# One statistics chain for the first tiles, upper parts written from x by VectorE, second halves normalised by ScalarE

## The chip, the core and the metric

The kernel runs on one core of one Trainium2 chip. The metric is the time of one execution on the device in microseconds (us). The engines of the core work side by side, each through its own instructions in order: TensorE (PE; its weight loads are shown apart as PEld), VectorE (DVE), ScalarE (ACT), GpSimd (POOL) and SyncE (SP), whose queue issues most of the DMAs.

## The reference

`x` has 2048 rows of 512. Its normalised rows go through two branches, and the product of these is added to `x`:

```
def reference(x, seq_re, seq_im, hid_re, hid_im, w1, b1, w2, b2):
    xn = (x - mean(x)) / sqrt(var(x) + 1e-5)          # over the 512 columns
    a, b = xn @ hid_re.T, xn @ hid_im.T
    s = seq_re @ a - seq_im @ b                       # seq: 2048 x 2048, hid: 512 x 512
    h = relu(xn @ w1 + b1) ** 2                       # 512 -> 1792
    g = silu(h @ w2 + b2)                             # 1792 -> 512
    return x + s * g
```

All of it is in float32.

## The kernel before

**Products of split numbers.** A float32 product is made of three products of float32r operands: each operand is split into an upper part (`HI`, the value written to a float32r tile, which rounds it) and a lower part (`LO`, the value minus its upper part), and upper x upper, upper x lower and lower x upper are summed in PSUM (`PASSES`, L98). `split_hi` (L133) is an ACT copy, `split_lo` (L136) a DVE subtraction.

**Chunks and steps.** The kernel first multiplies the sequence matrices with `xn`, in eight chunks of 256 output rows. A chunk has eight steps `j`; step `j` uses the tile pair `xr[j]`, rows 128 j and 1024 + 128 j onwards (the two halves `h` = 0 and 1), and a piece of the sequence matrices, loaded into `raw[c, j]` (tag `u`, three buffers) and split into `part[c, j]` (tags `ga`, `gb`). The first two chunks (`PLAIN`) are plain products: `products(c, j, h)` issues 12 matmuls of 128 x 512 for each half, four accumulators for each of the three passes, so 24 a step. In the first chunk the passes go one after the other over the four accumulators, so the lower parts are needed later than the upper. The later chunks use seven products of sums in place of eight (`PRODUCTS`); for these, `XC[j]` holds besides the four plain blocks also three blocks of sums of the blocks of `xn` (S2 to S4), and S1 in the place of a plain block.

**The first chunk also normalises.** While PE multiplies step `j`, the other engines prepare step `j + 1`. On DVE's and ACT's queues, step by step (L515 to L536):

- `ln_rstd(j)` (L223): from the root that ACT left, a RECIPROCAL and three small DVE operations make 1 / sqrt(var + eps) with one Newton step.
- `ln_xn(j, h)` (L232): DVE normalises each half into `xn32[j]` (tiles `wd0` for j = 0 to 3, `wd1` for 4 to 7); ACT writes the upper part of each into `XC[j]`.
- `split_lo(*g)`: DVE's lower part of this step's `g`; then `load_c` and some `load_x` on SP's queue, which wait until buffers are free.
- `split_lo` of `XC[j]`, half 0; then the statistics of tile `j + 1`: half 0 on DVE (`ln_stats`), half 1 on ACT (`ln_mean`, `ln_var`: a pass for the mean, one for the squares), and both roots by one ACT operation (`ln_root`); then `split_lo` of half 1.
- From `j = 5` on (`NJ - 3`), one item of `aside`; then the products; then ACT's upper part of the next `g`.

**The list `aside`** (L511) is work for later chunks, taken item by item: four sums over `xn32[0..3]` (`sums(0)`, DVE, 1024 columns), a split of the sums of each of these four tiles (`split_sums`: an ACT write of 768 columns, then a DVE subtraction), the same for tiles 4 to 7, and weights. What the first chunk doesn't take is taken beside the second chunk (`beside`, a budget of `ASIDE` for each step). `sums` writes in place over `xn32`, so it needs all four tiles of its group done and split.

**The start** (L475 to L506). PE is kept busy by 8 narrow-type and 6 float32r matmuls on zeros (`WARM`). For tile 0, each half has its own statistics and root; ACT splits the first half of `g`, DVE normalises, ACT writes the upper part from `xn32`, and the rest follows in an order written out by hand. All order here is the program's order: each engine runs its instructions as they are written.

Of the kernel before, what the change touches and what calls it, by code (L numbers as in the profile page):

```python
# [10 lines left out]
AF = mybir.ActivationFunctionType  # L11
ALU = mybir.AluOpType

P = 128
S, D, F = 2048, 512, 1792
NS, ND, NF = S // P, D // P, F // P
NJ, NP = NS // 2, NF // 2
# [1 line left out]
NC = S // CW  # L19
TC = 512  # L20
NTC = S // TC
WARM = 8, 6
PLAIN = 2

ASIDE = 3.6

REST = NP - 4

# [68 lines left out]
HI, LO = 0, 1  # L97
# [31 lines left out]
def fnet_gated_kernel(ctx, tc, x, xt, ct, wd, w1, w2, b1, b2, out):  # L129
    nc = tc.nc  # L130
    ctx.enter_context(tc.manual_schedule(engines=None))

    def split_hi(hi, lo, src):  # L133
        nc.scalar.activation(hi, src, AF.Copy)  # L134

    def split_lo(hi, lo, src):  # L136
        nc.vector.tensor_tensor(lo, src, hi.bitcast(F32), op=ALU.subtract)  # L137
# [5 lines left out]
    def copy(to, src, scale=1.0):  # L143
        nc.scalar.activation(to, src, AF.Copy, scale=scale)
# [8 lines left out]
    stats = pool.tile([P, 2, 2, NJ], F32, name="stats")  # L153
# [14 lines left out]
    def buf(tag, shape, name, dtype=F32):  # L168
        return pool.tile(shape, dtype, tag=tag, bufs=3 if tag == "u" else 1, name=name)

    def operand_buf(tag, name, step, shape=(2, 7, 256)):

        first = START.get(tag, 0)
        skip = (step - first) % 4 * LANE
        size = shape[0] * shape[1] * shape[2]
        room = ROOM.get(tag, 0)
        flat = buf(tag, [P, size + (room or skip)], name, F32R)
        a, b, c = shape
        return flat[:, skip:skip + size].rearrange("p (a b c) -> p a b c", a=a, b=b, c=c)

    def bcast(src, n):
        return bass.AP(tensor=src.tensor, offset=src.offset, ap=[[0, P], [1, n]])

    def halves(ap):
        return ap.rearrange("p (a b) -> p a b", a=2)


    XC = [None] * NJ
    for j in (0, 4, 5, 6, 7, 1, 2, 3):
        XC[j] = operand_buf(f"xc{j}", f"xc{j}", 3 if j in TURNED else 1, (7, 2, 256))  # L190
    small = buf("e", [P, 3, 16], "small")

    X_ROOM = "pq00", "pq01", "pq10", "pq11", "pq00", "pq01", "pq11", "pq00"
    xr, xn32 = {}, {}

    def load_x(j, hs=slice(0, 2)):

        if j not in xr:
            xr[j] = buf(X_ROOM[j], [P, 2, D], f"x{j}")
        nc.sync.dma_start(xr[j][:, hs], x.rearrange("(h j p) d -> j p h d", h=2, p=P)[j][:, hs])  # L200

    def ln_stats(j, h=0):
        bn = small[:, j % 3, 6 * h:6 * h + 6]
        nc.vector.bn_stats(bn, xr[j][:, h])
        nc.vector.bn_aggr(stats[:, :, h, j], bn)

    def ln_mean(j, h):

        nc.scalar.activation(junk, xr[j][:, h], AF.Copy, scale=1.0 / D, accum_out=stats[:, 0, h, j:j + 1])

    def ln_var(j, h):

        total = small[:, j % 3, 6 * h:6 * h + 1]
        nc.scalar.activation(junk, xr[j][:, h], AF.Square, bias=stats[:, 0, h, j:j + 1], scale=-1.0, accum_out=total)
        copy(stats[:, 1, h, j:j + 1], total, 1.0 / D)
# [3 lines left out]
    def ln_root(j, hs=slice(0, 2)):  # L219
        root[j] = small[:, j % 3, 12:16].rearrange("p (a h) -> p a h", a=2)  # L220
        nc.scalar.activation(root[j][:, 0, hs], stats[:, 1, hs, j], AF.Sqrt, bias=eps)

    def ln_rstd(j, hs=slice(0, 2)):  # L223
        y, q = root[j][:, 0, hs], root[j][:, 1, hs]
        var = rstd = stats[:, 1, hs, j]
        nc.vector.reciprocal(y, y)

        nc.vector.scalar_tensor_tensor(q, var, EPS, y, op0=ALU.add, op1=ALU.mult)
        nc.vector.scalar_tensor_tensor(q, q, -0.5, y, op0=ALU.mult, op1=ALU.mult)
        nc.vector.scalar_tensor_tensor(rstd, q, 1.5, y, op0=ALU.add, op1=ALU.mult)  # L230

    def ln_xn(j, h):  # L232
        if j % ND == 0 and h == 0:
            xn32[j, "tile"] = buf(f"wd{j // ND}", [P, ND, 2, D], f"xn32_{j}")
        if h == 0:
            xn32[j] = xn32[j // ND * ND, "tile"][:, j % ND]
        nc.vector.tensor_scalar(xn32[j][:, h], xr[j][:, h], stats[:, 0, h, j:j + 1], stats[:, 1, h, j:j + 1],
                                op0=ALU.subtract, op1=ALU.mult)

    def xc_parts(j, h):  # L240
        s = slice(2 * h, 2 * h + 2)
        return XC[j][:, s, HI, :], XC[j][:, s, LO, :], halves(xn32[j][:, h])
# [26 lines left out]
    def load_c(c, j, hs=slice(0, 2)):  # L269
        if (c, j) not in raw:  # L270
            raw[c, j] = buf("u", [P, 8, CW], f"u{c}_{j}")
        q = slice(2 * hs.start, 2 * hs.stop)
        nc.sync.dma_start(raw[c, j][:, q], ct[c, j, :, q])

    def plain_parts(c, j, hs=slice(0, 2)):
        if (c, j) not in part:
            part[c, j] = operand_buf("g" + "ab"[j % 2], f"g{c}_{j}", 0 if (c, j) == (PLAIN - 1, NJ - 1) else 3 if j in TURNED else 1, (2, 4, CW))
        g, r = part[c, j], raw[c, j]
        s = slice(2 * hs.start, 2 * hs.stop)
        return g[:, HI, s], g[:, LO, s], r[:, s]  # L280
# [87 lines left out]
    def products(c, j, h):  # L368

        for passes in [PASSES] if c else [[q] for q in PASSES]:  # L370
            for k in range(ND):
                one_product(c, j, h, k, passes)
# [8 lines left out]
    one, two = slice(0, 1), slice(1, 2)  # L381
# [95 lines left out]
    idle = buf("wd1", [P, 768], "idle")  # L477
    for count, zeros in zip(WARM, (idle[:, 0:256].bitcast(mybir.dt.bfloat16), idle[:, 256:768])):
        nc.vector.memset(zeros, 0.0)
        if zeros.dtype == F32:  # L480
            zeros = zeros.bitcast(F32R)
        for _ in range(count):
            nc.tensor.matmul(warm, zeros[:, 0:P], zeros, start=True, stop=True)
    for h, hs in enumerate((one, two)):
        ln_stats(0, h)
        ln_root(0, hs)
    split_hi(*plain_parts(0, 0, one))
    ln_rstd(0, one)
    ln_xn(0, 0)
    split_hi(*xc_parts(0, 0))  # L490
    split_lo(*plain_parts(0, 0, one))
    split_hi(*plain_parts(0, 0, two))
    ln_rstd(0, two)
    ln_mean(1, 1)
    ln_xn(0, 1)
    split_hi(*xc_parts(0, 1))
    split_lo(*xc_parts(0, 0))
    ln_stats(1)
    ln_var(1, 1)
    ln_root(1)  # L500
    split_lo(*plain_parts(0, 0, two))
    split_lo(*xc_parts(0, 1))
    g = plain_parts(0, 1)
    split_hi(*g)
# [9 lines left out]
    load_x(4)  # L514
    for j in range(1, NJ):  # L515
        ln_rstd(j)
        for h in range(2):
            ln_xn(j, h)
            split_hi(*xc_parts(j, h))
        split_lo(*g)  # L520
        load_c(*order[j + 3])
        if j in (1, 3, 4):
            load_x({1: 5, 3: 6, 4: 7}[j])
        split_lo(*xc_parts(j, 0))
        if j + 1 < NJ:
            ln_stats(j + 1)
            ln_mean(j + 1, 1)
            ln_var(j + 1, 1)
            ln_root(j + 1)
        split_lo(*xc_parts(j, 1))  # L530
        if j >= NJ - 3:
            next(aside)
        for h in range(2):
            products(0, j, h)
        g = plain_parts(*order[j + 1])
        split_hi(*g)  # L536
        if j == 2:
            nc.sync.dma_start(b1s, b1)
            nc.sync.dma_start(b2s, bcast(b2, D))
# [5 lines left out]
    def beside(spent):  # L545
        while spent < ASIDE:
            spent += next(aside, ASIDE)

# [47 lines left out]
    for n, s in enumerate(steps):  # L596
        c, j = s
# [3 lines left out]
        g = part.pop(s)  # L601
# [553 lines left out]
def _launch(arrays, out_shape):  # L1155
    import numpy as np
    import concourse.bacc as bacc
    from concourse.bass_utils import run_bass_kernel_spmd

    nc = bacc.Bacc("TRN2", target_bir_lowering=False, num_devices=1, dynamic_dma_scratch_size=1024)  # L1160
    feed, args = {}, []
    for name, v in arrays.items():
        v = np.ascontiguousarray(v)
        feed[f"in_{name}"] = v
        args.append(nc.dram_tensor(f"in_{name}", v.shape, mybir.dt.from_np(v.dtype), kind="ExternalInput").ap())
    args.append(nc.dram_tensor("out_0", out_shape, F32, kind="ExternalOutput").ap())
    with tile.TileContext(nc, schedule_with_timeline_sim=True) as tc:
        fnet_gated_kernel(tc, *args)
    r = run_bass_kernel_spmd(nc, [feed], core_ids=[0])
    return r.results[0]["out_0"]  # L1170
# [25 lines left out]
```

## Time and profile before

| | us |
|---|---|
| median of 3 runs | 673.32 |
| lowest and highest run | 673.16, 674.82 |
| span of the profiled execution | 671.8 |

The page gives the span of the profiled execution, and no time of its own for what lies around it; the median of the runs is 1.5 us longer than the span. The page has the busy time of each engine, then tenths of busy time in 40 slices, the DMA queues, the chain of work that ended last, and the costliest groups of instructions. A row of the timeline has start, duration, engine, line, operation, what it writes and reads, and in brackets the idle time of the engine before it with what ended that. A row with "x2" holds two instructions, and its duration reaches from the start of the first to the end of the last. On DVE and ACT an instruction can start shortly before the one ahead has ended, so the distance of two starts is what an instruction costs its queue. The granted clock of PE was full in all slices:

```profile
PEclk9999999999999999999999999999999999999999
```

### The profile page before, as it was taken

Reading aid. Unit: us, or ns where it says so; the run is one execution under the profiler, and the core shown is the slowest. Engines: PE = TensorE matmul, PEld = TensorE weight load, DVE = VectorE, ACT = ScalarE, POOL = GpSimd, SP = SyncE. Lnnn points to the kernel's source line nnn. Section 1 sums busy time; section 2 is a strip of 40 time slices with the busy share of each in tenths; the row PEclk is TensorE's granted clock in tenths of the full one; section 3 lists DMA queues with packets and bytes.
Section 4 is the critical chain, followed back from the end, with each engine's and each line's share of the span. In section 5 each row is a group of like instructions: output and inputs, shape, how many; then the busy total and the mean of one; then the engine's idle time right before and its main releaser. Section 6 shows DMA issues by size and latency. Waiting matters only on the chain.

```text
span 671.8 us, 13185 instructions
## 1 busy us (share of the span) xinstructions
PE 666.4 (99%) x5438; PEld 647.1 (96%) x5438; DVE 597.3 (89%) x833; ACT 379.0 (56%) x524; POOL 8.8 (1%) x11
## 2 busy tenths in 40 slices
PE   9999999999999999999999999999999999999997
PEld 6888889999999999999999999999999999999997
DVE  7997878999999999799899988977887889999997
ACT  6856554534445354444365557788778765454451
POOL 0000000000000000000000000000000000101010
PEclk9999999999999999999999999999999999999999
DMA  8625767646556774759588658676755866766776
GB/s 304 213 98 216 252 237 279 214 148 213 209 166 228 252 282 158 265 174 350 184 299 269 199 188 300 196 267 210 267 185 196 324 240 214 184 227 181 228 205 156
DMA packets 51739, 150.82 MB, mean 224 GB/s; under 512 B 4960, under 2 KB 19552, under 8 KB 50272
## 3 DMA queue, kind: packets, MB, share of 16 engines
q1 hardware_dynamic: 43568, 129.28, 56.5%
q10 hardware_dynamic: 6208, 18.88, 7.1%
q0 software_dynamic: 1904, 1.84, 1.9%
q8 instruction: 42, 0.69, 0.4%
q14 instruction: 17, 0.14, 0.1%
HBM read 101.98 MB, written 47.99 MB: 223 GB/s over the span
## 4 chain that ended last, share of the span: by engine, by line
PE 97%; DVE 1%; DMA 1%; ACT 0%; issue 0%; SPq 0%; DVEq 0%
PE m L362 34%; PE m_o L861 15%; PE r_B L755 13%; PE r_A L755 9%; PE pq_b L377 8%; PE r_C L755 4%; PE r_D L755 4%; PE m_last L861 4%; PE pq_ba L377 2%; PE pq_bc L377 2%; PE pq_bb L377 2%; DMA u<-in_ct 1%; DVE z L1111 0%; DVE z L911 0%; DVE z L916 0%
## 5 line engine op out<-in xcount | busy, mean ns | idle before, releaser
L362 PEld LDWEIGHTS m<-g,xc 128*128 128x128 f32 x2016 | 229.1, 188 | 0.1
L362 PE MATMUL m<-g,xc 128*128 128x256 f32 x2016 | 229.1, 276 | 0.0
L134 ACT ACTIVATE g<-u 128x1792 fp32r<-128x1792 f32 (+2 forms) x65 | 99.0, 1523 | 132.5 <-PE m L362 92.6
L137 DVE TENSOR_TENSOR g<-u,g 128x1792 fp32r<-128x1792 f32 (+2 forms) x65 | 116.9, 1798 | 19.8 <-ACT g L134 19.2
L861 PE MATMUL m_o<-w,g 128*128 128x256 f32 x882 | 100.5, 276 | 0.0
L861 PEld LDWEIGHTS m_o<-w,g 128*128 128x128 f32 x882 | 100.3, 188 | 0.0
L134 ACT ACTIVATE g<-hr 128x1792 fp32r<-128x1792 f32 (+2 forms) x31 | 48.2, 1566 | 40.0 <-DVE hr L296 15.3
L755 PE MATMUL r_B<-xT,w 128*128 128x256 f32 x504 | 66.5, 276 | 0.0
L377 PE MATMUL pq_b<-g,xc 128*128 128x512 f32 x240 | 65.3, 391 | 0.2 <-ACT xc L134 0.2
L755 PEld LDWEIGHTS r_B<-xT,w 128*128 128x128 f32 x504 | 61.4, 188 | 0.0
L137 DVE TENSOR_TENSOR g<-hr,g 128x1792 fp32r<-128x1792 f32 (+2 forms) x31 | 56.7, 1838 | 3.0 <-ACT g L134 2.8
L377 PEld LDWEIGHTS pq_b<-g,xc 128*128 128x128 f32 x240 | 44.8, 188 | 10.9 <-ACT xc L134 1.1
L755 PE MATMUL r_A<-xT,w 128*128 128x256 f32 x336 | 43.1, 276 | 0.0
L755 PEld LDWEIGHTS r_A<-xT,w 128*128 128x128 f32 x336 | 40.3, 188 | 0.2 <-DVE xT L137 0.2
L755 PE MATMUL r_B<-wdp,yg 128*128 128x256 f32 x288 | 35.8, 276 | 0.0
L284 DVE TENSOR_TENSOR u<-u 128x512 f32<-128x512 f32 x48 | 32.9, 685 | 2.4 <-DMA u<-in_ct 2.4
L755 PEld LDWEIGHTS r_B<-wdp,yg 128*128 128x128 f32 x288 | 34.1, 188 | 0.0
L861 PE MATMUL m_last<-w,g 128*128 128x256 f32 x294 | 33.5, 276 | 0.0
L861 PEld LDWEIGHTS m_last<-w,g 128*128 128x128 f32 x294 | 33.4, 188 | 0.0
L137 DVE TENSOR_TENSOR yg<-yraw,yg 128x1792 fp32r<-128x1792 f32 x13 | 26.2, 2018 | 0.6 <-ACT yg L134 0.6
L134 ACT ACTIVATE yg<-yraw 128x1792 fp32r<-128x1792 f32 x13 | 22.2, 1711 | 6.9 <-DVE yraw L293 6.4
L755 PE MATMUL r_D<-xT,w 128*128 128x256 f32 x168 | 23.6, 276 | 0.0
(187 smaller groups left out, 878.1 us busy)
## 6 DMA issues: line engine op xcount, KB each, us to landing
u<-in_ct SPq DMA_DIRECT2D x63, 512.0 KB, 3.8
hd<-h ACTq DMA_DIRECT2D x28, 512.0 KB, 4.2
hr<-hd SPq DMA_DIRECT2D x28, 512.0 KB, 3.7
wdp<-wdd SPq DMA_DIRECT2D x8, 896.0 KB, 6.2
yraw<-pqd SPq DMA_DIRECT2D x13, 512.0 KB, 6.3
pqd<-c SPq DMA_DIRECT2D x6, 1024.0 KB, 6.5
w<-w1d SPq DMA_DIRECT2D x6, 896.0 KB, 9.0
y<-y ACTq DMA_DIRECT2D x8, 512.0 KB, 6.1
```

Source lines behind the costliest of these rows:

```text
L134: nc.scalar.activation(hi, src, AF.Copy)
L137: nc.vector.tensor_tensor(lo, src, hi.bitcast(F32), op=ALU.subtract)
L284: nc.vector.tensor_tensor(t[:, 0:2], r[:, 0:1].to_broadcast([P, 2, 256]), r[:, 1:3], op=ALU.add)
L362: nc.tensor.matmul(ps[:, d], w[:, a_, d * P:(d + 1) * P], halves(mv(b_)), start=first and d == 0 and (a_, b_) == (HI, HI), stop=last and ( ...
L377: nc.tensor.matmul(accs[c][k], w, part[c, j][:, b_, 2 * h:2 * h + 2], start=j == 0 and h == 0 and (a_, b_) == (HI, HI), stop=j == NJ - 1 a ...
L755: nc.tensor.matmul(self.region(REGION[k]), w, mv, start=i == 0 and k in (1, 7), stop=i == len(ops) - 1, skip_group_check=True)
L861: nc.tensor.matmul(m[:, i * 256:(i + 1) * 256], ready[n][:, a_, H_SLOT[a], i * P:(i + 1) * P], W2[p][:, b_, b], start=p == 0 and i == 0 an ...
```

## The change

At the start, both halves of tile 0 have their statistics first, and then one root and one chain of small operations for both. A new function `ln_hi` lets DVE write an upper part straight from `x` (subtract the mean, multiply, write to `XC`), without going through `xn32`. A new function `ln_xn_act` lets ACT normalise a half into `xn32` as scale * x + bias, for which `ln_shift` makes the bias, minus mean times scale, on DVE. In step 0, both upper parts come from `ln_hi`, both halves of `xn32` from ACT. In step 1, the upper part of half 0 comes from `ln_hi`, both halves of `xn32` from ACT, and the lower part of `g` is made in two pieces. In steps 2 to 7, DVE normalises half 0 and ACT half 1, and ACT writes both upper parts from `xn32` as before. `SIDE` takes items of `aside` in step 4 (one) and in steps 5, 6 and 7 (two each) instead of one in each of 5, 6 and 7. One warm-up matmul goes.

```diff
-WARM = 8, 6
+WARM = 8, 5
...
+SIDE = {4: 1, 5: 2, 6: 2, 7: 2}
...
+    def ln_shift(j):
+
+        t = small[:, j % 3, 8:10]
+        nc.vector.scalar_tensor_tensor(t, stats[:, 0, :, j], -1.0, stats[:, 1, :, j], op0=ALU.mult, op1=ALU.mult)
+
+    def ln_xn_act(j, h):
+
+        xn32_tile(j, h)
+        nc.scalar.activation(xn32[j][:, h], xr[j][:, h], AF.Identity, scale=stats[:, 1, h, j:j + 1],
+                             bias=small[:, j % 3, 8 + h:9 + h])
+
+    def ln_hi(j, h):
+
+        nc.vector.tensor_scalar(XC[j][:, 2 * h:2 * h + 2, HI, :], halves(xr[j][:, h]), stats[:, 0, h, j:j + 1],
+                                stats[:, 1, h, j:j + 1], op0=ALU.subtract, op1=ALU.mult)
...
-    for h, hs in enumerate((one, two)):
-        ln_stats(0, h)
-        ln_root(0, hs)
+    for h in range(2):
+        nc.vector.bn_stats(small[:, 0, 6 * h:6 * h + 6], xr[0][:, h])
+    for h in range(2):
+        nc.vector.bn_aggr(stats[:, :, h, 0], small[:, 0, 6 * h:6 * h + 6])
+    ln_root(0)
+    ln_rstd(0)
+    ln_hi(0, 0)
+    ln_shift(0)
     split_hi(*plain_parts(0, 0, one))
-    ln_rstd(0, one)
-    ln_xn(0, 0)
-    split_hi(*xc_parts(0, 0))
+    split_hi(*plain_parts(0, 0, two))
     split_lo(*plain_parts(0, 0, one))
-    split_hi(*plain_parts(0, 0, two))
-    ln_rstd(0, two)
+    ln_xn_act(0, 0)
+    split_lo(*xc_parts(0, 0))
+    ln_hi(0, 1)
     ln_mean(1, 1)
-    ln_xn(0, 1)
-    split_hi(*xc_parts(0, 1))
-    split_lo(*xc_parts(0, 0))
+    ln_xn_act(0, 1)
     ln_stats(1)
     ln_var(1, 1)
+    split_lo(*plain_parts(0, 0, two))
     ln_root(1)
-    split_lo(*plain_parts(0, 0, two))
     split_lo(*xc_parts(0, 1))
...
     for j in range(1, NJ):
         ln_rstd(j)
-        for h in range(2):
-            ln_xn(j, h)
-            split_hi(*xc_parts(j, h))
-        split_lo(*g)
+        if j == 1:
+            ln_hi(j, 0)
+            ln_shift(j)
+            for h in range(2):
+                ln_xn_act(j, h)
+            split_lo(*plain_parts(0, j, one))
+            split_hi(*xc_parts(j, 1))
+            split_lo(*xc_parts(j, 0))
+            split_lo(*plain_parts(0, j, two))
+        else:
+            ln_shift(j)
+            ln_xn(j, 0)
+            ln_xn_act(j, 1)
+            for h in range(2):
+                split_hi(*xc_parts(j, h))
+            split_lo(*g)
+            split_lo(*xc_parts(j, 0))
         load_c(*order[j + 3])
...
-        split_lo(*xc_parts(j, 0))
...
         split_lo(*xc_parts(j, 1))
-        if j >= NJ - 3:
+        for _ in range(SIDE.get(j, 0)):
             next(aside)
```

More of the change, by code (lines that the diff above doesn't have):

```diff
@@ L230, in ln_rstd, with xn32_tile @@
         nc.vector.scalar_tensor_tensor(rstd, q, 1.5, y, op0=ALU.add, op1=ALU.mult)
+    def xn32_tile(j, h):
+        if j % ND == 0 and (j, "tile") not in xn32:
+            xn32[j, "tile"] = buf(f"wd{j // ND}", [P, ND, 2, D], f"xn32_{j}")
+        xn32[j] = xn32[j // ND * ND, "tile"][:, j % ND]
     def ln_xn(j, h):
[L233 to L236, printed above, removed]
+        xn32_tile(j, h)
         nc.vector.tensor_scalar(xn32[j][:, h], xr[j][:, h], stats[:, 0, h, j:j + 1], stats[:, 1, h, j:j + 1],
                                 op0=ALU.subtract, op1=ALU.mult)
+    def ln_shift(j):
+        t = small[:, j % 3, 8:10]
+        nc.vector.scalar_tensor_tensor(t, stats[:, 0, :, j], -1.0, stats[:, 1, :, j], op0=ALU.mult, op1=ALU.mult)
+    def ln_xn_act(j, h):
+        xn32_tile(j, h)
+        nc.scalar.activation(xn32[j][:, h], xr[j][:, h], AF.Identity, scale=stats[:, 1, h, j:j + 1],
[3 more added lines that the diff above has]
+                                stats[:, 1, h, j:j + 1], op0=ALU.subtract, op1=ALU.mult)
     def xc_parts(j, h):
```

## The prediction

> **What bounds the kernel now.** I read the page first, then the chain of work in order of time, then the waits of TensorE (PE), then VectorE (DVE) and ScalarE (ACT) row by row through the first 60 us, where the change lies.
>
> ```profile
> PE 666.4 (99%) x5438; PEld 647.1 (96%) x5438; DVE 597.3 (89%) x833; ACT 379.0 (56%) x524; POOL 8.8 (1%) x11
> ...
> PE warm L483 <- DVE idle L479: 1.2, 1, 1.2
> PE pq_b L377 <- ACT xc L134: 0.2, 1, 0.2
> ...
> 1.66 4.49 DMA u<-in_ct
> ...
> 6.17 0.63 ACT g L134
> 6.79 0.53 ACT xc L134
> ...
> 7.37 0.73 PE pq_b L377 x2
> ...
> 13.34 0.72 PE pq_b L377 x2
> ...
> 19.09 0.46 PE pq_b L377 x2
> ...
> 46.31 0.45 PE pq_b L377 x2
> ```
>
> The first row is busy time by engine; the next two are all the waits that PE has in the whole run, 1.2 us in front of the warm-up and 0.2 us at the first product; the rest are pieces of the chain (start, duration, what). The chain leaves the DMA of `u`, crosses two ACT splits, and is on PE from 7.37 us on. **So the time is the moment of PE's first product, plus what PE stands still, plus its work.** The most that a better start can give is small: the first product needs ACT's split of `u`, which starts at 6.17 us, so the gain there is under 1.2 us. What the change can lose has no such limit: each us that PE waits in the first chunk goes to the end, as nothing behind it waits today and so nothing gives way.
>
> Steps 2 to 7 of the first chunk take PE (46.31 - 19.09) / 5 = 5.44 us each. The question is whether the eight steps' operands still come in time. How far DVE and ACT are ahead today (start, duration, line, out<-in):
>
> ```profile
> 11.29 0.16 DVE L226 RECIPROCAL small<-small 128x2 f32<-128x2 f32 x1
> ...
> 16.12 0.16 DVE L226 RECIPROCAL small<-small 128x2 f32<-128x2 f32 x1
> ...
> 36.61 0.16 DVE L226 RECIPROCAL small<-small 128x2 f32<-128x2 f32 x1
> ...
> 37.39 1.00 DVE L237 TENSOR_SCALAR xn<-x,stats 128x512 f32<-128x512 f32 x2
> 38.31 1.22 DVE L137 TENSOR_TENSOR g<-u,g 128x1024 fp32r<-128x1024 f32 x1
> 39.44 0.69 DVE L137 TENSOR_TENSOR xc<-xn,xc 128x512 fp32r<-128x512 f32 x1
> 40.04 0.69 DVE L204 BATCH_NORM_STATS2 small<-x 128x6 f32<-128x512 f32 x1
> ...
> 40.87 0.66 DVE L137 TENSOR_TENSOR xc<-xn,xc 128x512 fp32r<-128x512 f32 x1
> 41.44 1.22 DVE L255 TENSOR_TENSOR xn<-xn 128x1024 f32<-128x1024 f32 x1
> 42.58 0.16 DVE L226 RECIPROCAL small<-small 128x2 f32<-128x2 f32 x1
> 43.36 1.00 DVE L237 TENSOR_SCALAR xn<-x,stats 128x512 f32<-128x512 f32 x2
> ...
> 43.94 1.16 ACT L134 ACTIVATE xc<-xn 128x512 fp32r<-128x512 f32 x2 [1.65 <-DVE xn L237]
> ```
>
> A step begins on DVE with its RECIPROCAL: step 1 at 11.29, 2 at 16.12, 6 at 36.61, 7 at 42.58 us. DVE has no gap between these rows. Step 7's first upper part is written by ACT at 43.94 + 0.61 = 44.55 us, and PE wants it at 46.31: **cover of 1.76 us at step 7**, with one sum (1.14 us from 41.44 to 42.58) in each of steps 5, 6 and 7.
>
> **The change part by part.**
>
> *The start.* Before, ACT wrote the first upper part behind the split of `u`; now DVE writes it from `x`.
>
> ```profile
> 3.52 0.69 DVE L204 BATCH_NORM_STATS2 small<-x 128x6 f32<-128x512 f32 x1 [1.82 <-DMA x<-in_x]
> ...
> 5.22 0.13 DVE L226 RECIPROCAL small<-small 128x1 f32<-128x1 f32 x1
> ...
> 5.97 0.55 DVE L237 TENSOR_SCALAR xn<-x,stats 128x512 f32<-128x512 f32 x1
> 6.17 0.63 ACT L134 ACTIVATE g<-u 128x512 fp32r<-128x512 f32 x1 [0.53 <-DMA u<-in_ct]
> ...
> 7.22 0.61 ACT L134 ACTIVATE g<-u 128x512 fp32r<-128x512 f32 x1
> ```
>
> One chain for both tiles: two statistics from 3.52, aggregates, one root, RECIPROCAL near 5.4, four small operations (5.22 to 5.97, 0.75) to 6.2, upper part by 6.75. The split of `u` ends at 6.80 and is last: first product near 6.85, 0.5 us sooner. The sixth wide warm-up matmul had to go for that. Dropping it costs nothing, since PE then has only a gap below 0.1 us.
>
> Behind it DVE forms the shift and one lower part, then waits for ACT's normalised half, which stands behind the second split of `u` (between 6.70, ACT free, and 7.22; I take 6.9) and ends near 8.25. Then lower part, upper part, statistics and two lower parts (0.60 + 0.46 + 0.82 + 1.20) bring step 1's RECIPROCAL to 11.4, against 11.29. **PE is 0.5 us earlier, DVE 0.1 us later.**
>
> *The normalisation on ACT.* No row has an ACTIVATE with two operands per partition (scale and bias). Nearest rows:
>
> ```profile
> 22.32 1.16 ACT L134 ACTIVATE xc<-xn 128x512 fp32r<-128x512 f32 x2 [0.51 <-DVE xn L237]
> 23.38 0.58 ACT L209 ACTIVATE junk<-x 128x512 f32<-128x512 f32 x1
> ...
> 24.97 0.20 ACT L144 ACTIVATE stats<-small 128x1 f32<-128x1 f32 x1
> 25.40 0.30 ACT L221 ACTIVATE small<-stats,eps 128x2 f32<-128x2 f32 x1 [0.23 <-DVE stats L205]
> ...
> L214 ACT ACTIVATE junk<-x,stats 128x512 f32<-128x512 f32 x7 | 4.8, 689 | 0.2
> L813 ACT ACTIVATE h<-h,b1s 128x512 f32<-128x512 f32 x10 | 7.1, 715 | 0.0
> ```
>
> A plain one takes 0.61 us, and the next starts 0.53 us after it; with one such operand it takes 0.69 to 0.715. If a second adds as much again, it is 0.77 to 0.82; I take 0.80, the next 0.71 later. The ends are 0.61 (free) and 0.82.
>
> In steps 2 to 7 ACT now runs: second half normalised (behind DVE's shift), both upper parts, mean, variance, root. From RECIPROCAL: 0.78 to the shift, 0.16 and a handover to 0.99, then 0.71 + 1.06 (two upper parts, 22.32 to 23.38) + 1.82 (23.38 to 25.17, and a handover) + 0.30 + 0.08 = **4.95 us to the next RECIPROCAL by ACT**. DVE's own: step 6 took 5.97, less a sum of 1.14, less one normalisation of 0.46, plus 0.08 for the shift = **4.45 us by DVE**. Without a sum the step is therefore 4.95, no shorter than the 4.83 it was: ACT's root is what is late next.
>
> Step 1 is longer, as both halves are on ACT and the shift stands behind DVE's upper part: 1.45 to ACT's start, 1.54 for two, 0.53, 1.82, 0.38 = 5.72. So step 2 starts at 11.4 + 5.72 = 17.1 instead of 16.12.
>
> Here a rule speaks against the change. The Trainium skill, "ScalarE: Activation LUTs", section "Rules for kernel authors", says that multiplying and adding belong on VectorE, not on ScalarE. The rows agree only where ACT sets the step: 0.46 us (37.39 to 38.31, two) leave DVE and some 0.71 come to ACT. By the rule kept, steps 2 and 3 would be 0.1 shorter, and steps 4 to 6, where DVE sets the pace, 0.38 longer each; so this move is not where the loss is.
>
> *The sums a step sooner.* `SIDE` puts seven items before step 7's end instead of three: one in step 4, two each in 5, 6 and 7. Their rows:
>
> ```profile
> 61.23 1.22 DVE L255 TENSOR_TENSOR xn<-xn 128x1024 f32<-128x1024 f32 x1
> 62.48 1.23 DVE L255 TENSOR_TENSOR xn<-s,xn 128x1024 f32<-128x1024 f32 x1
> ...
> 52.08 0.85 ACT L134 ACTIVATE xc<-xn 128x768 fp32r<-128x768 f32 x1
> ...
> 52.95 0.96 DVE L137 TENSOR_TENSOR xc<-xn,xc 128x768 fp32r<-128x768 f32 x1 [2.84 <-ACT xc L134]
> ```
>
> Sums back to back start 1.25 apart. Step 6's second item is a split: its ACT half needs the fourth sum, which DVE has just begun, and its DVE half needs ACT's. DVE stands still meanwhile, and behind it stands step 7's RECIPROCAL, with the lower parts of `g` and `xc`. Lengths: step 4, 4.45 + 1.14 = 5.59; step 5, 4.45 + 1.25 + 1.14 = 6.84; step 6, 4.45 + 1.27 (sum to its end) + 0.89 (ACT, 0.85 and a handover) + 0.87 = 7.48.
>
> *The sum.* Step 7's RECIPROCAL: 17.1 + 2 x 4.95 + 5.59 + 6.84 + 7.48 = 46.9, where it was 42.58. Its first upper part is 0.99 + 0.71 + 0.61 = 2.31 later, handed over at 49.3. PE began this step at 46.31: **PE starts step 7 about 3.0 us later**. Shorter waits at step 2 (17.1 + 2.3 = 19.4 against some 18.3) and step 6 are part of that and not added, and the 0.5 us gained at the start are waited away too.
>
> Behind step 7 nothing changes the sum: the lower part of the next `g` is due some 6.5 us after RECIPROCAL, at 53.4, and PE comes to it at 54.8. Four items fewer are left for the second chunk, where PE waits for nothing today, so nothing comes back. On SP's queue the loads of `u` keep their order and wait for the same DVE splits, up to 4.3 us later:
>
> ```profile
> u<-in_ct SPq DMA_DIRECT2D x12, 512.0 KB, 3.6
> ```
>
> 3.6 us to landing for a tile that is wanted two steps on: hidden. If that cover went, the next split of `u` on ACT would wait.
>
> The profiled span is 671.8 us; with 3.0 more it is 674.8. The median of the three runs shown, 673.32, lies 1.5 us above the span, so the forecast is **676.3 us**. Bounds: with the two-operand ACTIVATE as cheap as a copy, four of them in the way (two in step 1, one each in steps 2 and 3) and step 7's own give back 5 x 0.18 = 0.9, and an earlier second split of `u` 0.2: +1.9. At 0.82, with DVE's upper parts at 0.69 (the subtractions' row) for 0.55, it is +3.4: own range 675.2 to 676.8.
>
> **The rivals.**
>
> *ACT's chain doesn't bind* (not slower). Place: the root in steps 1 to 3. If each takes DVE's 4.45 us (mean, variance or root start before I think), step 7 begins at 11.4 + 3 x 4.45 + 19.91 = 44.7, and its upper part comes at 46.9 instead of 46.31: +0.6, **673.9 us**. It decides where ACT's part from shift to root falls from 3.9 to 3.4 us. For it: ACT is busy 56%. Against: the rows' own durations.
>
> *The start is kept.* If the covers of all steps suffice, the 0.5 us stay gained, and with them the short wait at 13.34 (0.72 us for two products against 0.45): -0.8, **672.5 us**. For it: the cover of 1.76. Against: four items of about 1.1 us against savings of 0.38 in three steps.
>
> *Not what it says: the functions share no table.* If Identity and Sqrt needed different tables, two loads would fall in each of seven steps:
>
> ```profile
> L465 ACT ACT_TABLE_LOAD x1 | 1.3, 1283 | 0.7 <-PEq L1160 0.7
> ```
>
> 7 x 2 x 1.28 = 18 us on ACT's chain, less some 3 of cover: **some 690 us**. Against: Sqrt, Square, Copy and Relu share the one load at L465. The Trainium skill, "ScalarE: Activation LUTs", section "Table sets: the hidden batching unit", has Identity among the functions of every set; no run here shows it.
>
> **How the numbers follow.** Forecast 0.73; ACT's chain doesn't bind 0.15; start kept 0.08; tables 0.02; other 0.02. The range is 673.6 to 677.2: it takes in the forecast's own range with some error on seven steps, and the first rival. A measurement of this kernel can tell about 0.3% (2.0 us) from no change. Nearly the whole forecast and the tables lie above it, less 0.07 for the forecast's low end: slower 0.69. Both other rivals and that end are within it: 0.29. Faster 0.02, as the start can't give 2 us.
>
> **What would show it.** In the profile after: PE's first product near 6.85; RECIPROCAL of step 2 near 17.1 and of step 7 near 46.9; waits of PE for `xc` at steps 2, 6 and 7, the longest (some 2 us) at step 7; DVE idle for about 0.9 us before step 6's split. I am wrong if step 7 begins on DVE before 45, if the new ACTIVATE is far from 0.80 us, or if PE waits past the first chunk.

## The result and the profile after

| | before | after |
|---|---|---|
| median of 5 runs, us | 673.32 | 677.92 |
| lowest and highest run, us | 673.06, 674.82 | 677.53, 679.50 |
| span of the profiled execution, us | 671.8 | 676.0 |

The ratio is 1.007 (95% interval 1.0058 to 1.0082): the change makes the kernel 0.7% slower, 4.6 us by the medians and 4.2 us by the two profiled spans. The forecast was slower, 676.3 us, with a range up to 677.2; the time lies 0.7 us above the range.

First all the waits of TensorE (PE), as the view of waits gives them for the kernel after (us in total, times, longest). Before the change there were two rows, 1.2 us at the warm-up and 0.2 us at the first product.

```profile
PE pq_b L397 <- ACT xc L136: 2.8, 3, 1.7
PE warm L503 <- DVE idle L499: 1.2, 1, 1.2
PE pq_b L397 <- DVE g L139: 0.5, 1, 0.5
PE pq_b L397 <- DVE small L247: 0.5, 1, 0.5
```

L136 and L139 are now the lines of the splits (upper part on ACT, lower part on DVE). The timeline of PE says where they fall (start, duration, what, and in brackets the idle time with its cause):

```profile
6.88 0.70 PE L397 MATMUL pq_b<-g,xc 128*128 128x512 f32 x2 [0.50 <-DVE small L247]
...
19.33 0.73 PE L397 MATMUL pq_b<-g,xc 128*128 128x512 f32 x2 [0.88 <-ACT xc L136]
...
41.57 0.73 PE L397 MATMUL pq_b<-g,xc 128*128 128x512 f32 x2 [0.16 <-ACT xc L136]
...
49.02 0.73 PE L397 MATMUL pq_b<-g,xc 128*128 128x512 f32 x2 [1.72 <-ACT xc L136]
```

PE's first product is at 6.88 us instead of 7.37. Not all of that is the change. In this execution the first piece of `u` landed sooner, so its split started at 5.27 us (6.17 before), and DVE's upper part was last:

```profile
5.27 0.63 ACT L136 ACTIVATE g<-u 128x512 fp32r<-128x512 f32 x1
...
6.19 0.55 DVE L257 TENSOR_SCALAR xc<-x,stats 128x512 fp32r<-128x512 f32 x1
```

Then PE waits for an upper part at step 2 (19.33), at step 6 (41.57) and longest at step 7: the product that stood at 46.31 us before stands at 49.02. A bracket is less than the whole loss, since the first matmuls after a wait also stand further apart (0.73 us for the pair, 0.62 in a running row) and a matmul's recorded end lies past the start of the next (0.39 us long, 0.23 from start to start). So the table counts by the starts of all matmuls. In a running row they are 0.227 us apart for 512 columns and 0.114 for 256; what a distance has beyond that is counted as lost, from 0.02 us on:

| stretch of the run, us | before | after |
|---|---|---|
| first product | 7.37 | 6.88 |
| lost up to 20 | 0.58 | 1.59 |
| lost, 20 to 54 (rest of the first chunk) | 0.00 | 2.42 |
| lost, 54 to 100 (second chunk) | 0.00 | 1.13 |
| lost after 100 | 0.41 | 0.38 |

The changes from before to after sum to -0.49 + 1.01 + 2.42 + 1.13 - 0.03 = 4.0 of the 4.2 us between the spans. The chain of step 6 on VectorE (DVE), which makes step 7 late:

```profile
39.20 0.16 DVE L228 RECIPROCAL small<-small 128x2 f32<-128x2 f32 x1
...
43.65 1.22 DVE L275 TENSOR_TENSOR xn<-xn 128x1024 f32<-128x1024 f32 x1
45.78 0.96 DVE L139 TENSOR_TENSOR xc<-xn,xc 128x768 fp32r<-128x768 f32 x1 [0.91 <-ACT xc L136]
46.66 0.16 DVE L228 RECIPROCAL small<-small 128x2 f32<-128x2 f32 x1
```

The fourth sum ends at 44.87; ScalarE (ACT) then writes its half of the split; DVE stands for 0.91 us, subtracts, and reaches step 7's RECIPROCAL at 46.66 instead of 42.58. ACT's side of the same stretch:

```profile
44.90 0.85 ACT L136 ACTIVATE xc<-xn 128x768 fp32r<-128x768 f32 x1 [0.84 <-DVE xn L275]
45.66 1.05 ACT L136 ACTIVATE g<-u 128x1024 fp32r<-128x1024 f32 x1
47.64 0.81 ACT L252 ACTIVATE xn<-x,small,stats 128x512 f32<-128x512 f32 x1 [0.94 <-DVE small L247]
48.36 2.61 ACT L136 ACTIVATE xc<-xn 128x512 fp32r<-128x512 f32 x4
```

Both engines wait for each other in turn. The first of the four writes at 48.36 is the upper part that PE waits for.

**The second chunk, which was not forecast.** DVE there, in the kernel after:

```profile
55.99 0.96 DVE L139 TENSOR_TENSOR xc<-xn,xc 128x768 fp32r<-128x768 f32 x1 [2.72 <-ACT xc L136]
56.87 1.22 DVE L275 TENSOR_TENSOR s<-xn 128x1024 f32<-128x1024 f32 x1
58.12 1.23 DVE L275 TENSOR_TENSOR xn<-xn 128x1024 f32<-128x1024 f32 x1
59.26 1.22 DVE L139 TENSOR_TENSOR g<-u,g 128x1024 fp32r<-128x1024 f32 x1
60.40 1.22 DVE L275 TENSOR_TENSOR xn<-s,xn 128x1024 f32<-128x1024 f32 x1
61.65 1.22 DVE L275 TENSOR_TENSOR xn<-xn 128x1024 f32<-128x1024 f32 x1
63.79 1.83 DVE L139 TENSOR_TENSOR xc<-xn,xc 128x768 fp32r<-128x768 f32 x2 [0.91 <-ACT xc L136]
65.53 1.22 DVE L139 TENSOR_TENSOR g<-u,g 128x1024 fp32r<-128x1024 f32 x1
```

The lower parts of `g` for steps 1 and 2 of the second chunk come at 59.26 + 1.22 = 60.48 and at 66.75 us, and PE loses 0.35 and 0.78 us for them (starts of matmuls). Where the `g` of step 1 waited behind one split, it now waits behind a split and two sums. Before the change the first group was a sum, done at 48.89 us, and a split; after the first `g`, three more splits and one sum came:

```profile
52.95 0.96 DVE L137 TENSOR_TENSOR xc<-xn,xc 128x768 fp32r<-128x768 f32 x1 [2.84 <-ACT xc L134]
54.87 1.23 DVE L137 TENSOR_TENSOR g<-u,g 128x1024 fp32r<-128x1024 f32 x1 [0.96 <-ACT g L134]
56.02 2.69 DVE L137 TENSOR_TENSOR xc<-xn,xc 128x768 fp32r<-128x768 f32 x3
58.62 1.22 DVE L255 TENSOR_TENSOR s<-xn 128x1024 f32<-128x1024 f32 x1
59.76 1.22 DVE L137 TENSOR_TENSOR g<-u,g 128x1024 fp32r<-128x1024 f32 x1
```

`beside` takes items until their listed costs reach 3.6. With four items gone from the front of the list, the groups are cut in other places: the first is now a split and two sums. It starts from 1.5, and 1.5 + 0.9 + 1.2 is 3.5999999999999996 in floating point, short of the budget by rounding, so a third item is taken. The second group puts the last sum directly in front of the split that needs it, and DVE and ACT wait for each other again (0.91 us at 63.79).

### The profile page after: what moved, and what is told of

It reads as the page before. It is cut to its first block, busy times and chain, and to the rows that moved or that the text cites. A ratio compares the mean times of both kernels' runs of the same rounds, so it can differ in the third digit from the quotient of the medians.

```text
span 676.0 us, 13189 instructions
## 1 busy us (share of the span) xinstructions
PE 666.8 (99%) x5437; PEld 646.2 (96%) x5437; DVE 594.6 (88%) x831; ACT 384.1 (57%) x530; POOL 8.8 (1%) x11
## 4 chain that ended last, share of the span: by engine, by line
PE 89%; DVE 7%; ACT 2%; DMA 1%; issue 1%; SPq 0%; DVEq 0%
PE m L382 34%; PE m_o L895 15%; PE r_B L789 13%; PE r_A L789 9%; PE r_C L789 4%; PE r_D L789 4%; PE pq_b L397 4%; PE m_last L895 4%; DVE xc L139 1%; PE pq_ba L397 1%; DVE g L139 1%; DVE xn L275 1%; DMA x<-in_x 1%; ACT xc L136 1%; DVE z L1145 0%
## 5 line engine op out<-in xcount | busy, mean ns | idle before, releaser
L136 ACT ACTIVATE g<-u 128x1792 fp32r<-128x1792 f32 (+2 forms) x65 | 99.0, 1523 | 129.5 <-PE m L382 93.5
L139 DVE TENSOR_TENSOR g<-u,g 128x1792 fp32r<-128x1792 f32 (+2 forms) x66 | 116.9, 1772 | 21.9 <-ACT g L136 21.4
L136 ACT ACTIVATE g<-hr 128x1792 fp32r<-128x1792 f32 (+2 forms) x31 | 48.2, 1566 | 39.9 <-PE m_o L895 16.7
L139 DVE TENSOR_TENSOR g<-hr,g 128x1792 fp32r<-128x1792 f32 (+2 forms) x31 | 56.7, 1838 | 2.9 <-ACT g L136 2.8
L139 DVE TENSOR_TENSOR yg<-yraw,yg 128x1792 fp32r<-128x1792 f32 x13 | 26.2, 2019 | 0.6 <-ACT yg L136 0.6
L136 ACT ACTIVATE yg<-yraw 128x1792 fp32r<-128x1792 f32 x13 | 22.2, 1707 | 5.5 <-DVE yraw L313 4.5
L146 ACT ACTIVATE r_B<-r_A 128x256 f32<-128x256 f32 x36 | 13.2, 368 | 18.3 <-PE r_A L789 9.7
```

## The experiments

Theory: the side work taken sooner makes step 7 late, above all by the split in step 6, and by its regrouping it also makes the second chunk late; two normalisations on ACT in step 1 make step 2 late, a loss that disappears inside the larger one at step 7. Rivals: ACT's normalisation is the loss, or late loads of `u` are. Each time is compared with the kernel before on the same chip.

### The new start and assignment with the old side work

```diff
-SIDE = {4: 1, 5: 2, 6: 2, 7: 2}
+SIDE = {5: 1, 6: 1, 7: 1}
```

> The changed kernel with one item of the side work in each of steps 5, 6 and 7 of the first chunk, as before the change. Theory (the side work taken sooner makes step 7 late and regroups the items of the second chunk; the new assignment of the normalisation costs little): VectorE begins step 7 near 42.9 us, TensorE waits only at step 2 (about 0.9 us) and nowhere later; step 7's first product near 46.7 us against 46.31 before; span about 672.2, time about 673.7 us. Rival (ScalarE's normalisation is the loss, the side work is hidden): step 7 late again, time near 677 us.

Measured: 674.09 us against 673.44 (ratio 1.001, 1.0001 to 1.002), span 672.6. RECIPROCAL of step 7 comes at 43.01, and PE's only long wait is at step 2:

```profile
PE pq_b L397 <- ACT xc L136: 0.9, 1, 0.9
PE pq_b L397 <- ACT g L136: 0.2, 1, 0.2
```

Of the 4.6 us some 3.9 go when the side work is put back. The rest of the change costs 0.1% by itself.

### The old kernel with the new side work

```diff
+SIDE = {4: 1, 5: 2, 6: 2, 7: 2}
...
-        if j >= NJ - 3:
+        for _ in range(SIDE.get(j, 0)):
             next(aside)
```

> The kernel before, with the side work of the change (one item in step 4, two each in steps 5, 6 and 7) and nothing else of it. Theory (side work): VectorE begins step 7 near 46.9 us, TensorE's first product of step 7 near 49.0 against 46.31, and about 1.1 us more of waits in the second chunk; span about 675.5, time about 677 us. Rival (ScalarE's normalisation is the loss): time near 673.5 us.

Measured: 678.39 us against 673.44 (1.0073, 1.0058 to 1.0088), span 676.6; the time is some 1.4 us above the expected one. The same wait of DVE stands in front of step 7, and its first product is as late:

```profile
46.28 0.96 DVE L139 TENSOR_TENSOR xc<-xn,xc 128x768 fp32r<-128x768 f32 x1 [0.91 <-ACT xc L136]
47.16 0.16 DVE L228 RECIPROCAL small<-small 128x2 f32<-128x2 f32 x1
...
49.20 0.74 PE L379 MATMUL pq_b<-g,xc 128*128 128x512 f32 x2 [2.08 <-ACT xc L136]
```

There are 1.15 us lost in the second chunk by the starts of the matmuls. Nothing of the new start or of ACT's normalisation is in this kernel, and it loses all of what the change loses. **The rival that ACT's normalisation is the loss falls** on these two runs.

This kernel has the old start and the old steps 1 to 3 unchanged. Its first split of `u` started at 5.34 us and its first product at 7.04, and it lost 1.20 us up to 20 us: 7.04 + 1.20 = 8.24, against 7.37 + 0.58 = 7.95 in the profile of the kernel before. So single profiles of one and the same start differ by 0.3 us.

### The first split out of step 6

```diff
-SIDE = {4: 1, 5: 2, 6: 2, 7: 2}
+SIDE = {4: 1, 5: 2, 6: 1, 7: 3}
```

> The changed kernel with the first split of the sums moved from step 6 to step 7: the same seven items by the end of step 7. Theory (VectorE's wait for ScalarE's half of that split, 0.9 us, and the split's own 0.87 us and the end of the sum ahead of it make step 7 late): step 7 begins on VectorE near 44.8 us, TensorE's wait of 1.7 us at step 7 goes or falls under 0.2; the waits of the second chunk stay near 1.1 us; span about 674, time about 675.8 us. Rival (the number of sums taken early is what counts, not the split): TensorE still waits over 1 us at step 7, time near 677.5 us.

Measured: 675.91 us against 673.44 (1.0038, 1.0023 to 1.0053), span 673.8. RECIPROCAL of step 7 at 44.37; no wait in the rows of step 7; 1.18 us lost in the second chunk. The same seven items are taken by the end of step 7, and PE loses 0.50 us from 20 to 54 us instead of 2.42, so the place of one split in the order is worth some 2 us. The four sums stand ahead of step 7 in both kernels, so they alone don't make its long wait; the split behind them does. Step 6 takes DVE 5.59 us here instead of 7.46: 0.91 of the difference is DVE's wait for ACT, the rest is the split itself and the end of the sum before it. Whether another fifth item, without such a wait, would also be too much was not tried.

### The budget of the second chunk

```diff
-ASIDE = 3.6
+ASIDE = 3.59
```

> The changed kernel with the budget of the side work in the second chunk at 3.59 instead of 3.6, so that 1.5 + 0.9 + 1.2 (3.5999999999999996 in floating point) ends the first group there, which takes three items in the changed kernel and two with this. Theory (the regrouped items put VectorE late for the lower parts of g in the second chunk): the waits of TensorE near 60 and 66 us, 1.1 us in sum, go; the first chunk stays as it is, with 1.7 us of waiting at step 7; span about 674.9, time about 676.8 us. Rival (the loads of u, issued up to 4 us later, land late in the second chunk): the waits stay, time near 677.9 us.

Measured: 676.81 us against 673.44 (1.0055, 1.004 to 1.007), span 674.8; the loss in the second chunk is 0.00 by the starts of the matmuls, and step 7's wait is still 1.68 us. DVE in the second chunk of this kernel:

```profile
56.28 0.96 DVE L139 TENSOR_TENSOR xc<-xn,xc 128x768 fp32r<-128x768 f32 x1 [2.69 <-ACT xc L136]
57.15 1.22 DVE L275 TENSOR_TENSOR s<-xn 128x1024 f32<-128x1024 f32 x1
58.29 1.22 DVE L139 TENSOR_TENSOR g<-u,g 128x1024 fp32r<-128x1024 f32 x1
```

One sum fewer stands in front of `g`, which comes at 59.51 instead of 60.48. A hundredth in a budget is worth 1.1 us here: **the cut of the groups makes the second chunk's waits**, and the rival of late loads falls: the loads of this kernel are ordered as in the changed one, and in the changed kernel ACT, which splits every `u`, has no wait for a DMA between 14 and 110 us.

### What makes step 2 late

Three kernels with the new start. The first undoes ACT's normalisation in steps 2 to 7, with the old side work:

```diff
-SIDE = {4: 1, 5: 2, 6: 2, 7: 2}
+SIDE = {5: 1, 6: 1, 7: 1}
...
         else:
-            ln_shift(j)
-            ln_xn(j, 0)
-            ln_xn_act(j, 1)
             for h in range(2):
+                ln_xn(j, h)
                 split_hi(*xc_parts(j, h))
```

> The new start and the new step 1, but steps 2 to 7 normalised as before (both halves on VectorE), and the side work as before (one item in each of steps 5, 6, 7). Theory (the two normalisations that step 1 gives to ScalarE make its root late, and that alone makes TensorE wait at step 2): RECIPROCAL of step 2 near 17.0 us, later ones 4.84 apart, a wait of about 0.6 us at step 2 and none later; time about 673.8 us. Rival (the normalisation that steps 2 to 7 give to ScalarE makes the wait): no wait at step 2, time near 672.8 us.

Measured: 673.55 us against 673.25 (1.0002, 0.9994 to 1.0011). RECIPROCAL of step 2 at 17.18, the next three 4.84 apart, a wait of 0.55 us at step 2 (19.23), none later. The wait stays with the old steps 2 to 7: **it is made in step 1.**

The second also gives one of step 1's two normalisations back to DVE:

```diff
         if j == 1:
...
-            for h in range(2):
-                ln_xn_act(j, h)
+            ln_xn_act(j, 0)
+            ln_xn(j, 1)
```

> As the run before (new start, steps 2 to 7 and side work as before), but in step 1 only half 0 is normalised by ScalarE, half 1 by VectorE. Theory (one normalisation fewer, 0.71 us and the wait for its end, in front of ScalarE's root): RECIPROCAL of step 2 near 16.2 us, no wait of TensorE at step 2 or later; the gain of the start is kept: span about 671.2, time about 672.7 us, 0.6 to 0.7 below the kernel before. Rival (VectorE's longer step 1 takes the place of ScalarE's): RECIPROCAL of step 2 past 16.6, TensorE waits at step 2, time 673.3 or more.

Measured: 672.68 us against 673.25 (0.9993, 0.9984 to 1.0001). No wait at step 2 or at any later step of the two first chunks, as the theory has it; but RECIPROCAL of step 2 came at 16.62 in the profiled execution, as the rival has it, because step 1 already began at 11.63 there (behind ACT, which had waited 0.96 us for `x`), and PE lost 0.58 us at step 1 (starts of the matmuls) instead. That execution was the slowest of the eleven, 673.99 us. Step 1 on DVE took 4.99 us from one RECIPROCAL to the next, against 5.70 in the changed kernel.

The third keeps ACT's normalisation in steps 2 to 7 (only `SIDE` as before and the step 1 above):

> As the run before, but steps 2 to 7 with the second half normalised by ScalarE, as the change has it; side work as before. Theory (with ScalarE's root ending a step of 4.90 us and TensorE's step of 5.44, the assignment costs nothing once step 2 is in time): RECIPROCAL of step 2 near 16.2 us, then 4.90 apart up to step 5; no wait at step 2 or later; time within 0.3 us of the run before, about 672.7 us. Rival (the assignment costs by itself): waits of TensorE in steps 2 to 7, time over 673.2 us.

Measured: 673.62 us against 673.25 (1.0004, 0.9995 to 1.0013), 0.9 above the run before it. **A miss.** The RECIPROCALs of steps 2 to 4 are 4.90 apart as expected (from 16.38 on, not 16.2, and 5.04 from step 4 to step 5), and step 2 loses only 0.28 us (its upper part stands behind the normalisation on ACT). A wait at step 2 and a time above 673.2 us are what the rival has. Its losses up to 20 us are 0.74 us, and none from there to 100; after 100 us it lost 0.77 against the 0.41 of the kernel before, in places that the change doesn't touch. What makes the rest of the 0.9 us stays open; the kernel of the run before, timed once more below (`e10_one_half_again`), is at 673.02, so some of it is the spread of the times.

### The four sums early and no split

The same step 1, ACT's normalisation in steps 2 to 7, and one item in each of steps 4 to 7:

```diff
-SIDE = {4: 1, 5: 2, 6: 2, 7: 2}
+SIDE = {4: 1, 5: 1, 6: 1, 7: 1}
```

> As the run before, with one item of the side work in each of steps 4 to 7: the four sums a step sooner and no split of them in the first chunk. Theory (the normalisation moved to ScalarE pays for one sum in a step, and only the split and the second sum of a step break the cover): RECIPROCAL of step 7 near 42.9 us, its first upper part near 45.2, no wait of TensorE at step 7 or later; time about 672.7 us. Rival (any item taken sooner is late for TensorE): a wait at step 7 or in the second chunk, time 673.3 us or more.

Measured: 674.77 us against 673.25 (1.002, 1.0011 to 1.0029). Half a miss. RECIPROCAL of step 7 at 42.57 and no loss of PE from 20 to 54 us: in the first chunk the moved normalisation does pay for a sum a step sooner (from step 4 to step 7 it is 16.77 us with three sums here, and 16.77 with two in the profile of `e10_one_half_again`, where DVE normalises both halves). But the second chunk loses 1.42 us by the starts of the matmuls, with the brackets in these rows of PE:

```profile
57.20 2.11 PE L397 MATMUL pq_b<-g,xc 128*128 128x512 f32 x8 [0.20 <-DVE g L139]
...
69.08 2.11 PE L397 MATMUL pq_b<-g,xc 128*128 128x512 f32 x8 [0.47 <-DVE g L139]
```

One item fewer at the front is enough to cut the groups badly again: three splits before the first `g` here.

### A version that keeps the start's gain

The version with one half on ACT in step 1, and one with the start changed further (DVE also normalises half 1 of tile 0, and its upper part is written while DVE waits for ACT's half 0), on one chip:

```diff
     ln_xn_act(0, 0)
-    split_lo(*xc_parts(0, 0))
     ln_hi(0, 1)
+    split_lo(*xc_parts(0, 0))
     ln_mean(1, 1)
-    ln_xn_act(0, 1)
+    ln_xn(0, 1)
     ln_stats(1)
```

> The version with one normalisation on ScalarE in step 1, and in the start VectorE also normalises half 1 of tile 0; its upper part of half 1 moves into the 0.4 us in which VectorE waited for ScalarE's half 0. Theory (TensorE's waits in the first 20 us are set by ScalarE's root for tile 1, which stands behind this normalisation): RECIPROCAL of step 1 near 10.9 to 11.2 us with no wait for the root, TensorE's wait at step 1 (0.4 to 0.5 us) under 0.15; time about 672.3 us, 0.3 to 0.4 below the version before it. Rival (the landing of x for tile 1 sets it): RECIPROCAL of step 1 past 11.3, time as the version before it.

> The version with one normalisation on ScalarE in step 1 again, beside the run before on one chip. Theory (the start's gain of 0.5 us is kept once step 2 is in time and the side work is as before): median 0.4 to 0.7 us below the kernel before. Rival (its first time was chance): no difference to the kernel before, within 0.2 us.

Measured, against 673.18 of the kernel before: 672.98 with the further change (0.9996, 0.9988 to 1.0005), 673.02 without (0.9995, 0.9986 to 1.0004). The further change brings nothing that can be measured: no wait for the root remains, but RECIPROCAL of step 1 came at 11.51 in its profile, behind work of DVE, later than the 10.9 to 11.2 expected; the time is that of the version before it, as the rival has it, though no engine waits for `x` there. Both profiles show PE's losses up to 20 us and the first product summing to less than the 7.95 us of the kernel before: 7.05 + 0.62 = 7.67 and 6.92 + 0.42 = 7.34. A gain of 0.3 to 0.6 us is in these traces, but two profiles of the old start differ by 0.3 us among themselves, and the times lie 0.2 us (0.6 in its first trial) below the kernel before, with intervals that all reach 1. Whether it beats the kernel before is left open; it is some 5 us below the changed kernel.

## Why the prediction was wrong

- **What bounds the kernel** held: 4.0 of the 4.2 us between the spans are places where PE stands still.
- **The start** came out right in its number by luck (first product at 6.88, forecast 6.85). The forecast had the split of `u` end last, at 6.80; it ended at 5.27 + 0.63 = 5.90, and DVE's upper part ended last, at 6.19 + 0.55 = 6.74. The bound of 1.2 us also came from one execution in which `u` was late: the old start reached 7.04 when `u` came sooner. PE stood 0.50 us idle before the first product, not under 0.1, and the granted clock stayed full. RECIPROCAL of step 1 came at 11.25 (forecast 11.4), but behind ACT's root, where the forecast had DVE's own work last; ACT had waited 0.68 us for `x`.
- **The ACTIVATE with two operands** was taken at 0.80 us from rows with one. The group of ten after the change:

```profile
L252 ACT ACTIVATE xn<-x,small,stats 128x512 f32<-128x512 f32 x10 | 8.0, 812 | 4.4 <-DVE small L247 4.2
```

  0.812 us, inside the bounds of 0.61 and 0.82.
- **Step 1 and ACT's chain** held: step 1 took 5.70 us (5.72), with RECIPROCAL of step 2 at 16.95 (17.1), of step 3 at 21.86 and of step 4 at 26.76, 4.9 apart (4.95). "ACT's root is what is late next" is in the rows, for instance this one of DVE:

```profile
21.86 0.17 DVE L228 RECIPROCAL small<-small 128x2 f32<-128x2 f32 x1 [0.37 <-ACT small L223]
```

- **The sums and the split** in the first chunk held: steps 4, 5 and 6 took 5.60, 6.84 and 7.46 us (5.59, 6.84, 7.48); step 7 began on DVE at 46.66 (46.9), and PE's first product of it stood at 49.02 (49.3).
- **The failed step** is the one behind step 7: "Four items fewer are left for the second chunk, where PE waits for nothing today, so nothing comes back." I counted the items that are left and not how they fall into groups. That PE waits for nothing there was true of the old grouping only. The term was set at nothing, and it is 1.13 us; the budget run takes it away and nothing else, and the old kernel gets it too with the new side work. I also bounded the sum only by durations in the first chunk, so the range had no room for it; without these 1.13 us the time would have been 676.8, inside the range. The prediction names a wait of PE past the first chunk as a sign of being wrong, and it is the sign that came; the other two, step 7 before 45 us and an ACTIVATE far from 0.80, did not.
- **The rest of the miss** is the offset. I laid 1.5 us between the span and the median of before, which pairs the span of one execution with the times of others. Where both are shown for one execution, the kernel before has 1.7 to 1.8 us between them (33 executions beside `e5_steps_as_before`), and the changed kernel 1.9 to 2.0. Why the changed kernel has more around its span stays open. For the profiled execution, 677.92 - 676.0 = 1.9, it is 0.4 more than I laid; with the 1.1 us this makes 1.5 of the 1.6 us between forecast and median.
- **Small slips of the sums** change nothing in this: ACT's step adds up to 4.96 us, not 4.95; the upper end of the forecast's own range, 3.4 us over the kernel before, is 676.7, not 676.8; the tables' 18 us less 3 make 688, not 690.
- **The rivals.** "ACT's chain doesn't bind" fell: the RECIPROCALs of steps 2 to 4 stand behind ACT's root. "The start is kept" fell for this change; in the versions that leave the side work alone it shows as far as single profiles and times whose intervals reach 1 can show it. "The functions share no table" fell: the profile after has two table loads, as before, the second in the last part of the run. So here the trace agrees with the Trainium skill, "ScalarE: Activation LUTs", section "Table sets: the hidden batching unit", which has Identity in every set. The rule of the Trainium skill, "ScalarE: Activation LUTs", section "Rules for kernel authors", to multiply and add on VectorE, was weighed as not being where the loss is, and that held. The move itself made 0.46 us on DVE into 0.72 on ACT (17.94 to 18.66 us), and with the move kept and the old side work 0.65 of the 4.6 us are left. Undoing the move in steps 2 to 7 as well left 0.30, on another chip and with overlapping intervals, so what the move costs by itself is not shown.

## What to carry to other kernels

Where one engine is busy for 99% of the span, look at how far each step's operands are ahead of it, and spend no more side work in a step than that cover; two engines that hand one item to and fro cost the sum of their times in the queue, not the longer one (DVE stood 0.91 us in front of step 7, and again at 63.79 us). When items are moved out of a list that is cut by a budget, write down the new groups of all later cuts, and mind that a budget that is met exactly on paper can be missed by rounding. The gain at the start was worth nothing here, since later steps made PE wait. And take the distance between a span and a time from one execution, not from two.

## What was not expected of the hardware

DVE's TENSOR_SCALAR of 128x512 with a float32r result costs no more than the same with a float32 result. The group rows after the change:

```profile
L241 DVE TENSOR_SCALAR xn<-x,stats 128x512 f32<-128x512 f32 x6 | 3.3, 542 | 0.0
L257 DVE TENSOR_SCALAR xc<-x,stats 128x512 fp32r<-128x512 f32 x3 | 1.6, 545 | 0.1
```

542 and 545 ns, although the second writes two blocks of 256 apart from each other. That made 0.69 us, the upper bound that I had put, too high.
